# Attention and gated MLP on one core: the order of issue of all five engines is replaced

## The chip, the cores and the metric

The kernel runs on one core of one Trainium2 chip. The metric is the device time of one execution in microseconds (us), taken as the median of several executions. Five engines of the core matter: PE (TensorE: matmuls and transposes), DVE (VectorE), ACT (ScalarE), Pool (GpSimd, used here almost only to start transfers that add into what lies in SBUF), and SP (SyncE, which starts loads and stores). Each takes its instructions strictly in the order in which they were issued to it.

## What is computed

Attention over 8 batches of 8 heads, 576 tokens and 64 columns, then an MLP over the 4608 tokens of width 512. All inputs and outputs are fp32.

```python
def _attn_ref(q, k, v):
    q_d = q.reshape(B, H, Sd, factor, D).mean(axis=3)      # factor = 4, Sd = 144; k_d, v_d alike
    ...
    out_d = sm_attn(q_d, k_d, v_d)                         # full softmax attention of 144 x 144
    out_up = np.repeat(out_d, factor, axis=2)
    mask = np.abs(pos[:, None] - pos[None, :]) < factor    # a band of 7 keys for each token
    scores = np.where(mask, scale * np.matmul(q, k.transpose(0, 1, 3, 2)), -1000000.0)
    ...                                                    # softmax
    return out_up + np.matmul(attn, v)

def _moe_ref(x, w1, w2, w3, w_out):
    a = x @ w1
    b = x @ w2
    h = a * b @ w3
    return h @ w_out
```

## The kernel before

Every fp32 product of the MLP is made of three products of fp32r halves: a matrix is split into a rounded high half and the rest, its low half (`three()`, L310 to L312: high times high, high times low, low times high). w3 and w_out are first multiplied with each other (`fold`, products at L414, result split into `wphl`, L430), so that the MLP has three matrices left: two of gates and one down.

**Units and chunks.** Each batch is cut into 3 units of 192 tokens, 24 in all, and two units make a chunk of 384, 12 in all. `unit(n)` (batches 2 to 7) computes the band attention on DVE and ACT: seven products `pr` of q with shifted k (L860), their sums over 64 columns `s` (ACT L870, DVE L873), a softmax (L885 to L895), and seven products `pv` of weights and shifted v (ACT L918, DVE L926). The first of them is the accumulator `xl`. Three of the other six are added to it by DVE (L936) and three by a transfer that Pool starts and that adds in SBUF (L934), by turns, so each of Pool's additions stands between two of DVE's. There are 54 of them. Then `xl` is transposed (`xt`, L940), the pooled attention is added (L947) and x is split into `xh` and `xl` (L953, L954). The batches 0 and 1 take another way in groups (`pooled_sums`, `group_unit`, `group_scores` L745, `rest`, `group_values` L788), with PE making scores and values and DVE the sums of the softmax (`esm`, L770 to L772).

**Pooled attention.** `pooled(b)` needs sums of four neighbouring rows of q, k and v. SP loads the first quarter (`qks` L489, `vs` and `vl` L492 to L494) and Pool adds the three others by transfers (`qks` L507; v at L491 in three pieces, 72 and 56 rows into `vs` and 16 into `vl`). Each addition into a piece waits for the one before it into the same piece. `vl` is copied once by DVE for batches 0 and 1 (L511). `quad` then makes scores, exponentials and values on PE and ACT (L568, L583, L607, L529).

**Chunks of the MLP.** `moe(c)` runs over 8 slices of the hidden width. For each slice PE makes two gate products into `pab` (L310 to L312), ACT copies one (`a`, L1008), DVE multiplies the other in (L1010), ACT makes the high half `gh` (L1015) and DVE the low half `gl` (L1017). PE multiplies both down into `acc`, three banks at once; ACT copies them out (`o_sb`, L1029) and SP stores them (L1045, L1047).

**What sets the order.** All steps are first recorded in a `Plan` as tasks, each with its engine, its inputs and the buffers that it takes; `BUFS` says how many buffers each kind of tile has (3 `kv`, 3 `pv`, 2 `xl`, 1 `vs`, 1 `qks`). Then the table `ORDER` (L63 to L164) says for each engine in which order it takes its tasks. A number in it is the task's place in the order of recording on that engine:

```python
left[e] = [l[k] for w in ORDER[e].split() for a, _, b in [w.partition("-")] for k in range(int(a), int(b or a) + 1)][::-1]
```

The five orders are merged into one program order by a cost model in `Plan.order`; on each engine the order is the table's. The weights come as raw words through 4 buffers (`raw`, `words()`), which DVE and ACT convert (DVE L354, L357) and join, so SP's next weight load waits for a join.

Of the kernel before, what the change touches and what calls it, by code (L numbers as in the profile page):

```python
# [64 lines left out]
        "64 63 65-66 68 67 69 71 70 72-74 76 75 77-79 3 80 4 81-82 7 2 84 83 5 1 86 85 11 9 0 87 14 10 88-89 24 27 26 25 94 28 31 29 95 "  # L65
        "30 90 92 91 32 96 93 8 6 97-98 34 100 99 17 33 39 37 36 15 38 22 35 101 13 19 23 45 16 20 102 43 103 12 105 41-42 44 40 104 106 "
        "46 48 47 112 111 21 114-115 49 113 50 116 51 117 53-54 18 52 120 118-119 122 121 123 55 57-58 125 124 56 60 126 59 128 127 "
        "130-131 129 61 109 132-133 62 107 135 139 134 153 136 177 138 137 154 140 174 141 155 175 173 142 182 156 172 180 157 176 110 "
        "178 108 181 179 183 144 143 146 196-197 149 199 198 145 159 147-148 150 158 151 202 152 204-205 203 200 206 209 207-208 210-211 "
        "187 160 189 186 161 185 188 184 212 216 213-214 217 215 163 218 223 222 220-221 219 191 190 193 226 225 224 194 192 162 195 201 "  # L70
        "227-233 165 164 257 256 234 258 265 264 259-260 254 266 255 166 261 269 267 263 262 270 268 167 274 278 281 280 275 271 279 273 "
        "168 276 282 277 272 169 283-284 170 285 287 286 171 288-289 235 310 236 313 312 237 311 238-239 317 315 314 337 341 338 316 340 "
        "342 339 241 348 344-345 347 318 343 346 349 240 243 350-351 242 320-321 324 352 325 323 322 353-354 245 356 355 357-358 367 359 "
        "368 360 365 364 363 244 361 370 247 371 246 372 366 373 248 374 369 319 330 328 249 375 250 327 331 376-377 251 326 309 378 329 "
        "379-380 290 381 408 332 382-384 333 385 252 386 334 292 409 291 410 413 387 411 335 414 412 294 293 336 253 418 417 416 419 415 "
        "295 435 438 436 296 420 297 421-423 298 465 424-425 466 437 362 463 426 300 427-428 464 429 473 442 299 469 301 462 467 471 430 "
        "441 302 440 431-432 470 468 472 304 439 303 388 305 474-475 306 476 307 443 477-480 389 507 445 450 446 444 449 481 510 448 509 "
        "391 447 390 508 512 511 453 308 393 452 392 482 456 518 455 433 454 483-486 451 517 515 514 394 513 516 395 519 434 520-521 397 "
        "522 459 523-525 396 399 457 526-528 458 398 538 536 539 534 529 540 460-461 537 542 530 533 400 535 487 401-402 544 541 531 543 "
        "579 582 545 403 581 404 580 546-550 488 585 583 551 405 584 552 609 586 553 490 489 554 587 555 491 556-557 607 613 492 611 606 "  # L80
        "616 608 610 406-407 494 589 617 493 593 590 615 612 614 591-592 496 618 532 594 495 619-623 498 624 634 497 625-630 500 633 599 "
        "635 632 640 637 596 588 499 638 600 636 502 501 595 558 639 641 643 503 642 597-598 644 603 645 559 646-650 682 677 651 560-561 "
        "680 602 504 562 678 652 563 679 653 601 654-655 685 578 656 681 565 505-506 604-605 684 683 686 688 704-706 564 707 687 709 711 "
        "689-690 567 710 566 691-693 708 694-695 731 734 569 631 712 735 696-697 733 568 571 736 739 738 698 570 714 719 715 699-701 713 "
        "740 572 732 657 742 573-574 737 716 718 741 575-576 743 717 658-659 744-746 660 723 577 780 747 661 748-749 781 662 778 750-751 "
        "722 725 752-753 724 754-755 787 720 664 779 663 777 721 776 726 784 727 782 702 665-666 786 785 728 783 703 667 788 668 789-793 "
        "670 806-807 669 794-795 805 729-730 796-800 802 671-672 808 756 673 803 809 804 810 674 813 812 811 757 814-816 675 759 817 "
        "848-849 818 850 819 851 758 761 821 760 852 676 820 876 822-825 763 880 855 854 877 826 853 875 856 886 762 879 878 885 882 765 "
        "881 883-884 887 764 801 767 858 863 888-891 766 859 769 894-895 860 896-897 857 768 862 861 892-893 898 771 905 903 770 868 865 "
        "901-902 772 827 899 906 773-774 869 866 904 867 864 828 911 907-908 910 830 912 872 909 829 913 832 847 775 871 914-915 831 "  # L90
        "916-918 920 834 951 921 947 919 950 870 833 953 955 922-923 948 924-925 949 836 954 873 946 874 956 835 838 957 837 952 958 973 "
        "975-976 840 974 839 959-960 900 961 841 979 965-966 1001 977 967 842 968 978 926 843 1002 1004 980 962-963 1000 964 969 1003 "
        "981-982 1005 1009 927 1006-1007 844 970 1010 845 929 1008 846 1011 928 930-931 983 988 986 1012 984 1013-1015 985 987 1016 933 "
        "1050 932 993 934 1019 972 991 1046 1017 1048 1018 1020 1047 935 990 1052 1021-1022 936 1023 1049 1051 1024 971 992 937 989 1054 "
        "1056 1053 1045 1055 939 994 996 995 1057 938 940 997 941 998-999 1058-1060 942 1025 1061-1063 943-944 1064-1065 1076 1066-1067 "
        "1026 1075 1068 1080 1028 945 1073 1069 1027 1029 1081 1079 1030 1074 1078 1072 1071 1082 1031-1032 1077 1083-1085 1034 1033 "
        "1086-1088 1090 1089 1091 1036 1092-1095 1035 1037 1070 1038-1041 1096-1097 1099 1042-1043 1098 1101 1044 1100 1103 1102 1105 "
        "1104 1107 1106 1108-1109 1111 1110 1112-1114"
    ),
    DVE=(  # L100
        "71-75 1-2 5-7 77 76 78-79 3 0 4 80 22 8-10 81-83 12 11 13 15-16 23-25 29 14 30-32 36 17 85 84 86 19-20 37-39 21 87 18 43 88-89 "
        "52 90 26 51 53 91 54-55 44 56 96 92 94 97 93 58 57 59 98-99 45 33-34 46 100 27 60-62 35 101 28 102 50 103-106 40 111 113 95 112 "
        "41 115 114 116 42 47-49 117-118 180 63 119-120 64-65 122 181 123 121 184 66 124 185-186 125 67 127 126 68 165 69 129 128 70 166 "
        "130 179 107 182 167 172 183 173 136 131 174 168 175 149 132 134 201 133 150 195 135 137 202 151 190-192 138 109 194 196 198 197 "
        "108 153 169 110 187 208 170-171 199 176 139 177 209 178 188 193 141-142 152 200 140 189 215 144 143 220-222 146-147 145 154 148 "
        "223-225 216-217 155 203-204 156 226-228 157 205-207 229-230 210 231 211 219 212-213 159 214 158 218 232-234 252-255 160 259-262 "
        "161 266-269 256 273-274 257 235 258 275-276 263-265 162-163 270 164 271 280 272 281-282 277-279 283-287 304 236 305-306 237 "
        "307-308 238 316 318 320 239 319 317 321 323 322 309 240 324 326-327 325 328-330 242 331-332 311 241 333 310 312 336 243 345 347 "
        "349 244 313-315 334-335 348 338 246 346 350 352 245 337 339 248 351 247 353 355 354 341 356 249 357-358 250 359 340 251 360-362 "
        "389 391 364 393 390 363 366 288 392 342 394 396 289-290 367 365 395 397 399 291 369 400 292 398 401-403 418-420 368 293 430 294 "  # L110
        "431-432 404 295 405-406 433-436 343 437 296 344 370 421-422 409 407-408 371 423 298 297 411 299 438 440 412 300 410 414 439 "
        "441-444 301-302 372 303 445 413 446-447 450 448 475 477 479 424-426 476 449 373 480 478 482 481 427-428 374-375 415-416 377 429 "
        "483 485 452-453 376 451 486 484 455 378 487-488 379 454 489-491 494 503-505 492 380 507 381 506 493 508 510 417 456 383 382 "
        "496-497 509 548 457 549 384 511 385 513-514 550 512 495 386 515-517 499 387 458 388 518-521 498 523 551 560 552 562 564 561 553 "
        "459 565 500 522 461 566 563 462 567 525 460 526 555 554 463 524 556 568 528 570-571 501 569 465 527 572 464 573-577 589 466 578 "
        "557 467 591 590 593 558 580 579 468 592 469 594 596 502 582 595 529 471 581 470 530 597 599 472 583 585 473 598 474 559 600 531 "
# [1062 lines left out]
```

## Time and profile before

| | us |
|---|---|
| median of 3 runs | 765.7 (765.47 to 766.26) |
| the profiled execution, whole | 765.72 |
| span of its instructions | 763.9 |
| PE busy | 745.8 (98%) |
| DVE busy | 604.1 (79%) |
| ACT busy | 534.2 (70%) |
| Pool busy | 128.7 (17%) |
| granted TensorE clock, mean | 0.995 |

The times of the rows are of the profiled execution, in us from the start of its span. "Busy" counts instructions, not what they wait for. A row of a timeline says when an instruction starts, how long it takes and, in brackets, how long its engine had been idle before it and what released it. A chain of waits goes back from the last instruction, at each step to what released it; "issue" is time in which the engine waited for nothing that the profile shows. The granted clock is a share of full speed: 1.00 is 2.4 GHz, half of it 1.2 GHz.

### The profile page before, as it was taken

Reading aid. Unit: us, or ns where it says so; the run is one execution under the profiler, and the core shown is the slowest. Engines: PE = TensorE matmul, PEld = TensorE weight load, DVE = VectorE, ACT = ScalarE, POOL = GpSimd, SP = SyncE. Lnnn points to the kernel's source line nnn. Section 1 sums busy time; section 2 is a strip of 40 time slices with the busy share of each in tenths; the row PEclk is TensorE's granted clock in tenths of the full one; section 3 lists DMA queues with packets and bytes.
Section 4 is the critical chain, followed back from the end, with each engine's and each line's share of the span. In section 5 each row is a group of like instructions: output and inputs, shape, how many; then the busy total and the mean of one; then the engine's idle time right before and its main releaser. Section 6 shows DMA issues by size and latency. Waiting matters only on the chain.

```text
span 763.9 us, 14865 instructions
## 1 busy us (share of the span) xinstructions
PE 745.8 (98%) x5288; PEld 647.4 (85%) x5288; DVE 604.1 (79%) x1063; ACT 534.2 (70%) x2133; POOL 128.7 (17%) x163
## 2 busy tenths in 40 slices
PE   9999999999999998999999899999999999999995
PEld 5445788889999997899998799898999989999995
DVE  4856995649999997999999788999989989775121
ACT  5698778567887786878788677877885966852211
POOL 2030030300221222112122112102132211010000
PEclk9999999999999999999999999999999999999998
DMA  9988952653776577657585558755778365332101
GB/s 311 304 230 271 272 144 72 131 156 130 142 163 176 131 147 163 155 127 162 157 158 130 148 135 187 143 138 137 153 168 193 73 145 122 94 63 42 42 1 42
DMA packets 51462, 111.89 MB, mean 146 GB/s; under 512 B 5548, under 2 KB 19884, under 8 KB 51388
## 3 DMA queue, kind: packets, MB, share of 16 engines
q0 software_dynamic: 15360, 38.94, 30.2%
q1 hardware_dynamic: 35892, 71.75, 29.0%
q8 instruction: 41, 0.67, 0.4%
q14 instruction: 33, 0.27, 0.1%
q10 hardware_dynamic: 136, 0.26, 0.1%
HBM read 80.26 MB, written 9.44 MB: 117 GB/s over the span
## 4 chain that ended last, share of the span: by engine, by line
PE 68%; DMA 18%; DVE 5%; issue 5%; ACT 2%; POOL 1%; SPq 0%; POOLq 0%; DVEq 0%; ACTq 0%
PE pab L310 14%; PE pab L312 14%; PE pab L311 14%; PE acc L312 7%; PE acc L310 7%; PE acc L311 7%; DMA vs<-in_v_dram 4%; DMA raw<-in_w_dram 4%; DMA xl<-pv 3%; DMA vl<-in_v_dram 2%; DMA q<-in_qk_dram 2%; DMA qks<-in_qk_dram 2%; PE o_ps L529 2%; PE s_ps L568 1%; PE t_ps L607 1%
## 5 line engine op out<-in xcount | busy, mean ns | idle before, releaser
L918 ACT ACTIVATE pv<-kv,s 128x64 f32<-128x64 f32 x432 | 114.9, 338 | 19.5 <-DVE s L895 18.8
L870 ACT ACTIVATE junk<-pr 128x64 f32<-128x64 f32 x432 | 110.4, 255 | 17.5 <-DVE pr L860 8.1
L860 DVE TENSOR_TENSOR pr<-q_t,kv 128x768 f32<-128x768 f32 x126 | 116.5, 948 | 4.5 <-DMA kv<-in_kw_dram 4.0
L312 PE MATMUL acc<-wphl,gl 128*128 128x512 f32 x288 | 113.8, 395 | 3.2 <-DVE gl L1017 3.2
L310 PE MATMUL acc<-wphl,gh 128*128 128x512 f32 x288 | 114.5, 397 | 0.5 <-ACT gh L1015 0.5
L311 PE MATMUL acc<-wphl,gh 128*128 128x512 f32 x288 | 113.0, 392 | 0.0
L934 POOL DMA_DIRECT2D xl<-pv x54 | 48.8, 903 | 321.4 <-DVE xl L936 262.4
L1008 ACT COPY a<-pab 128x384 f32<-128x384 f32 x96 | 45.3, 472 | 68.4 <-PE pab L312 53.7
L873 DVE TENSOR_REDUCE s<-pr 128x12 f32<-128x768 f32 x90 | 84.1, 946 | 0.4
L1010 DVE TENSOR_TENSOR a<-pab,a 128x384 f32<-128x384 f32 x96 | 52.9, 551 | 39.4 <-PE pab L312 36.5
L870 ACT ACTIVATION_READ_ACCUMULATOR junk<-pr 128x1 f32 x432 | 81.1, 188 | 0.0
L1017 DVE TENSOR_TENSOR gl<-a,gh 128x384 fp32r<-128x384 f32 x96 | 52.7, 550 | 28.8 <-ACT gh L1015 28.7
L1015 ACT CAST gh<-a 128x384 fp32r<-128x384 f32 x96 | 48.7, 508 | 35.5 <-PE acc L311 23.2
L926 DVE TENSOR_TENSOR pv<-kv,s 128x768 f32<-128x768 f32 x72 | 67.7, 950 | 5.1 <-DMA xl<-pv 4.6
L312 PEld LDWEIGHTS acc<-wphl,gl 128*128 128x128 f32 x288 | 54.3, 188 | 16.1 <-DVE gl L1017 4.5
L310 PE MATMUL pab<-xh,wo 128*128 128x384 f32 x192 | 65.1, 339 | 1.5 <-ACT a L1008 1.5
L310 PE MATMUL pab<-xh,w1a 128*128 128x384 f32 x192 | 66.0, 344 | 0.0
L310 PE MATMUL pab<-xh,wb 128*128 128x384 f32 x192 | 65.9, 343 | 0.0
L491 POOL DMA_DIRECT2D vs<-in_v_dram x48 | 49.4, 1096 | 93.5 <-DMA vs<-in_v_dram 92.4
L310 PE MATMUL pab<-xh,w2a 128*128 128x384 f32 x192 | 65.2, 339 | 0.0
L312 PE MATMUL pab<-xh,wb 128*128 128x384 f32 x192 | 64.8, 337 | 0.0
L311 PE MATMUL pab<-xl,wb 128*128 128x384 f32 x192 | 64.7, 337 | 0.0
(120 smaller groups left out, 1754.5 us busy)
## 6 DMA issues: line engine op xcount, KB each, us to landing
xl<-pv POOLq DMA_DIRECT2D x54, 384.0 KB, 4.3
raw<-in_w_dram SPq DMA_DIRECT2D x32, 512.0 KB
qks<-in_qk_dram POOLq DMA_DIRECT2D x18, 576.0 KB, 7.4
kv<-in_kw_dram SPq DMA_DIRECT2D x18, 576.0 KB
kv<-in_vw_dram SPq DMA_DIRECT2D x18, 576.0 KB
out_dram<-o_sb SPq DMA_DIRECT2D x29, 256.0 KB
q_t<-in_q_dram SPq DMA_DIRECT2D x18, 384.0 KB
raw<-in_wout_dram SPq DMA_DIRECT2D x8, 512.0 KB
```

The source lines that it names most:

```text
L310: nc.tensor.matmul(out_ps, lhsT=lh, rhs=rh, start=first, stop=False)
L311: nc.tensor.matmul(out_ps, lhsT=lh, rhs=rl, start=False, stop=False)
L312: nc.tensor.matmul(out_ps, lhsT=ll, rhs=rh, start=False, stop=last)
L491: dma = (lambda **kw: nc.gpsimd.dma_start(accum_op=ALU.add, **kw)) if add else nc.sync.dma_start
L860: (nc.gpsimd if o in share["qk_pool"] else nc.vector).tensor_tensor(out=T[o], in0=T["q"], in1=T["k"][:, o * D:o * D + nq].rearrange("p (t ...
L870: nc.scalar.activation(out=junk, in_=T[o][:, t], func=AF.Copy, accum_out=T["s"][:, t, o:o + 1])
L873: reds.append(add("DVE", dve_us(nq), lambda o=o: nc.vector.tensor_reduce(out=T["s"][:, :, o], in_=T[o], op=ALU.add, axis=AX.X), [tp], uses ...
L918: nc.scalar.mul(out=T["pv", o][:, tt], in_=T["v"][:, (tt + o) * D:(tt + o + 1) * D], mul=T["s"][:, tt, o:o + 1])
L926: nc.vector.tensor_tensor(out=T["pv", o], in0=T["v"][:, o * D:o * D + nq].rearrange("p (t d) -> p t d", d=D), in1=T["s"][:, :, o].unsqueez ...
L934: t = add("Pool", 0.9, lambda o=o: nc.gpsimd.dma_start(out=T["x"], in_=T["pv", o], accum_op=ALU.add), [t, tm], uses=[hx, h], late=dma_us(1 ...
L1010: tg = add("DVE", dve_us(CT), lambda f=f: nc.vector.tensor_tensor(out=T["a", f], in0=T["p", 1, f], in1=T["a", f], op=ALU.mult), [ta, ends[ ...
L1017: tl = add("DVE", dve_us(CT), lambda f=f: nc.vector.tensor_tensor(out=T["gl", f], in0=T["a", f], in1=T["gh", f].bitcast(F32), op=ALU.subtr ...
```

## The change

Only the numbers in `ORDER` change, in all five lists. No task is added, removed or given to another engine. Moved are 594 of 807 tasks of PE, 913 of 1037 of DVE, 1028 of 1115 of ACT, 127 of 146 of Pool and 104 of 174 of SP, most of them by a few places. The first line of two lists:

```diff
     Pool=(
-        "0 2 5 3 1 4 6 9 7-8 13 12 16 10 15 18 11 19 14 17 23 20 27 21 31 24-25 28 41 29 32 45 33 22 26 34 30 35 49 36-37 42-43 38 44 48 "
+        "0 3 1-2 5-6 4 9 8 7 10 13 16 11 14 12 15 19 17-18 20-21 24 28 23 22 26 25 29 27 31 41 45 30 32 49 33-37 43-44 48 38 52 42 62 39 "
...
     SP=(
-        "13-16 0-1 17-20 2 21-22 3-5 23-26 12 27-38 6-7 39-40 8-9 41 59 42-43 60 10-11 44-46 56-57 47-48 61 64 58 62-63 68 49-52 81 65-67 "
+        "13-16 0 17-18 1 19-20 2 21-22 3-5 23-26 12 27-37 59 6-8 38-41 9-11 42-44 56 60 45-46 62 61 47-48 63 57-58 65 64 49-50 68 51-52 "
```

What the order looks like at four places follows. A row is one instruction, with its line, its kind, the tiles out<-in and the shape; the number behind a tile's name tells tiles apart within one kernel, and the two kernels number differently.

Pool at the start, the nine accumulations of batch 0's pooled v (`vs` in pieces of 72 and 56 rows, `vl` of 16 rows), before:

```order
L491 DMA vs_296<-in_v4_dram 56x512 x2
L491 DMA vl_297<-in_v4_dram 16x512
L491 DMA vs_296<-in_v4_dram 72x512 x2
L491 DMA vl_297<-in_v4_dram 16x512 x2
L491 DMA vs_296<-in_v4_dram 72x512
L491 DMA vs_296<-in_v4_dram 56x512
```

And after:

```order
L491 DMA vl_298<-in_v4_dram 16x512
L491 DMA vs_297<-in_v4_dram 72x512
L491 DMA vs_297<-in_v4_dram 56x512 x2
L491 DMA vl_298<-in_v4_dram 16x512
L491 DMA vs_297<-in_v4_dram 72x512
L491 DMA vl_298<-in_v4_dram 16x512
L491 DMA vs_297<-in_v4_dram 56x512
L491 DMA vs_297<-in_v4_dram 72x512
```

Of the three chains the short one on `vl` now starts first, and between two issues into the same piece stands an issue into another, except for one pair of 56 rows.

DVE at the start, around its copy of `vl` (L511); `raw`, `w3` and `wx` are weights being converted and joined, `esm` and `se` the softmax of a score group, `gsm` and `pexp` the pooled softmax. Before:

```order
L771 RECIPROCAL esm_271<-esm_271 128x6
L590 TENSOR_SCALAR gsm_497<-gsm_497 128x6
L591 RECIPROCAL gsm_497<-gsm_497 128x6
L598 TENSOR_TENSOR pexp_85<-pexp_85,gsm_497 128x3x16
L772 TENSOR_TENSOR se_322<-se_322,esm_324 128x432
L354 TENSOR_SCALAR raw_473<-raw_473 128x512
L772 TENSOR_TENSOR se_269<-se_269,esm_271 128x432
L357 SCALAR_TENSOR_TENSOR w3_562<-w3_562,raw_473 128x512
L511 COPY vl_297<-vl_297 16x512
L357 SCALAR_TENSOR_TENSOR w3_580<-w3_580,raw_535 128x512
L357 SCALAR_TENSOR_TENSOR w3_604<-w3_604,raw_541 128x512
L354 TENSOR_SCALAR raw_553<-raw_553 128x512
```

And after:

```order
L770 TENSOR_SCALAR esm_326<-esm_326 128x6
L771 RECIPROCAL esm_326<-esm_326 128x6
L511 COPY vl_298<-vl_298 16x512
L770 TENSOR_SCALAR esm_386<-esm_386 128x6
L771 RECIPROCAL esm_386<-esm_386 128x6
L772 TENSOR_TENSOR se_384<-se_384,esm_386 128x432
L770 TENSOR_SCALAR esm_269<-esm_269 128x6
L771 RECIPROCAL esm_269<-esm_269 128x6
L772 TENSOR_TENSOR se_267<-se_267,esm_269 128x432
L354 TENSOR_SCALAR raw_560<-raw_560 128x512
L357 SCALAR_TENSOR_TENSOR w3_621<-w3_621,raw_480 128x512
```

The copy stood among joins of weights; now the sums of two score groups stand directly behind it and the joins behind those.

DVE around the second of Pool's three additions into unit 9's `xl`. The first row is DVE's second addition into this unit's `xl`, which Pool's transfer follows, and the last row is DVE's third, which needs that transfer; `pr` and `s1` belong to unit 10, `gl` and `a` to the gates of a chunk. Before:

```order
L936 TENSOR_TENSOR xl_3393<-xl_3393,pv_3503 128x768
L873 TENSOR_REDUCE s1_80<-pr_3610 128x12
L873 TENSOR_REDUCE s1_80<-pr_3598 128x12
L926 TENSOR_TENSOR pv_3688<-kv_2991,s0_79 128x768
L1017 TENSOR_TENSOR gl_3683<-a_3580,gh_3682 128x384
L885 TENSOR_REDUCE mx_3705<-s1_80 128x12
L887 TENSOR_TENSOR s1_80<-s1_80,mx_3705 128x12x7
L1010 TENSOR_TENSOR a_3703<-pab_3601,a_3703 128x384
L936 TENSOR_TENSOR xl_3393<-xl_3393,pv_3635 128x768
```

And after, where DVE's second addition into this `xl` stands two rows above the first row shown:

```order
L926 TENSOR_TENSOR pv_3673<-kv_3016,s0_79 128x768
L926 TENSOR_TENSOR pv_3683<-kv_3016,s0_79 128x768
L954 TENSOR_TENSOR xl0_3644<-xt_3476,xh0_3643 128x4x192
L873 TENSOR_REDUCE s1_80<-pr_3613 128x12
L885 TENSOR_REDUCE mx_3717<-s1_80 128x12
L887 TENSOR_TENSOR s1_80<-s1_80,mx_3717 128x12x7
L1010 TENSOR_TENSOR a_3689<-pab_3663,a_3689 128x384
L892 TENSOR_REDUCE sm_3725<-s1_80 128x12
L894 RECIPROCAL sm_3725<-sm_3725 128x12
L895 TENSOR_TENSOR s1_80<-s1_80,sm_3725 128x12x7
L1017 TENSOR_TENSOR gl_3661<-a_3593,gh_3660 128x384
L936 TENSOR_TENSOR xl_3511<-xl_3511,pv_3673 128x768
```

Between the two additions there were seven rows, four of them long (two sums, one product, one `gl`); now there are twelve, among them two products, the `xl` of a finished unit, one sum and two `gl`.

Pool between 390 and 425 us of the trace; `xl_4786` before and `xl_4827` after are unit 13's accumulator, `xl_5084` and `xl_5203` unit 14's, and `vs_4993`, `vl_4994` before and `vs_4819`, `vl_4820` after are batch 5's pooled v. Before:

```order
L934 DMA xl_4786<-pv_4727 128x768
L507 DMA qks_4257<-in_qk4_dram 128x1152
L934 DMA xl_4786<-pv_4811 128x768
L934 DMA xl_4786<-pv_4956 128x768
L491 DMA vl_4994<-in_v4_dram 16x512
L491 DMA vs_4993<-in_v4_dram 72x512
L491 DMA vl_4994<-in_v4_dram 16x512 x2
L491 DMA vs_4993<-in_v4_dram 56x512 x2
L934 DMA xl_5084<-pv_5171 128x768
L934 DMA xl_5084<-pv_5265 128x768
```

And after:

```order
L934 DMA xl_4827<-pv_4751 128x768
L491 DMA vs_4819<-in_v4_dram 56x512
L491 DMA vs_4819<-in_v4_dram 72x512 x2
L934 DMA xl_4827<-pv_4922 128x768
L491 DMA vl_4820<-in_v4_dram 16x512 x2
L934 DMA xl_4827<-pv_5013 128x768
L934 DMA xl_5203<-pv_5115 128x768
L491 DMA vl_4820<-in_v4_dram 16x512
L507 DMA qks_5185<-in_qk4_dram 128x1152
L934 DMA xl_5203<-pv_5256 128x768
```

Unit 14's first addition stood behind six accumulations of v; now it stands directly behind unit 13's last one, and three accumulations into `vs` have moved ahead of unit 13's second addition.

## Rows read from the trace of the kernel before

**Rows 1.** The page's table of busy time, first line.
```profile
PE 745.8 (98%) x5288; PEld 647.4 (85%) x5288; DVE 604.1 (79%) x1063; ACT 534.2 (70%) x2133; POOL 128.7 (17%) x163
```
**Rows 2.** Stretches: length, busy PE, PEld, DVE, ACT, POOL, clock, DMA share, GB/s.
```profile
8.50:90.00 81.50, 78.48 (x632) 39.76 (x633) 60.06 (x151) 62.56 (x167) 7.65 (x9) 1.00 0.92 285
...
290.00:312.00 22.00, 19.97 (x157) 16.53 (x156) 17.59 (x27) 14.70 (x66) 4.37 (x5) 1.00 0.72 136
...
420.00:436.00 16.00, 13.33 (x88) 11.57 (x81) 11.07 (x17) 9.77 (x44) 2.54 (x3) 0.89 0.50 126
...
570.00:630.00 60.00, 59.34 (x404) 53.23 (x403) 52.99 (x87) 43.63 (x194) 11.90 (x14) 1.00 0.60 139
...
700.00:764.00 64.00, 56.20 (x293) 51.82 (x291) 13.61 (x23) 12.22 (x25) 0.00 (x0) 0.97 0.09 25
```
**Rows 3.** PE's waits: line, what it waited for, us in total, times, longest.
```profile
PE acc L312 <- DVE gl L1017: 3.2, 3, 2.7
...
PE se_ps L745 <- DMA k<-in_qk_dram: 0.8, 1, 0.8
PE oe_ps L788 <- DMA v_w<-in_v_dram: 0.8, 1, 0.8
PE se_ps L745 <- DVE se L756: 0.7, 2, 0.4
```
**Rows 4.** The chain of waits, 405 to 440 us: start, length, what.
```profile
414.89 1.12 POOL vs L491
416.01 3.87 issue
...
420.42 8.34 DMA xl<-pv
...
433.37 0.43 PE acc L311
...
436.08 0.23 PE acc L311
```
**Rows 5.** DVE's timeline, 414 to 434 us: start, length, instruction, wait ahead.
```profile
415.58 0.95 DVE L926 TENSOR_TENSOR pv<-kv,s 128x768 f32<-128x768 f32 x1
...
428.78 0.96 DVE L926 TENSOR_TENSOR pv<-kv,s 128x768 f32<-128x768 f32 x1 [4.04 <-DMA xl<-pv]
```
**Rows 6.** DVE's timeline, 286 to 306 us.
```profile
297.96 0.96 DVE L936 TENSOR_TENSOR xl<-xl,pv 128x768 f32<-128x768 f32 x1 [3.96 <-DMA xl<-pv]
```
**Rows 7.** The chain of waits of the whole span, two of its transfers.
```profile
263.20 4.27 DMA xl<-pv
...
290.01 7.93 DMA xl<-pv
```
**Rows 8.** DVE's timeline, 49 to 63 us.
```profile
59.13 0.42 DVE L511 COPY vl<-vl 16x512 f32<-16x512 f32 x1 [4.04 <-DMA vl<-in_v_dram]
```
**Rows 9.** Pool's timeline, 33 to 60 us.
```profile
37.45 0.84 POOL L491 DMA_DIRECT2D vs<-in_v_dram  x1 [2.90 <-DMA vs<-in_v_dram]
```
**Rows 10.** Stretches of the start, as in rows 2.
```profile
55.00:60.00 5.00, 5.00 (x20) 2.69 (x19) 0.93 (x3) 4.98 (x13) 2.25 (x3) 1.00 0.71 169
```
**Rows 11.** DVE's timeline, 654 to 657 us.
```profile
654.85 0.95 DVE L954 TENSOR_TENSOR xl<-xt,xh 128x768 fp32r<-128x768 f32 x1
```
**Rows 12.** PE's timeline, 655.8 to 656.6 us.
```profile
656.20 0.33 PE L310 MATMUL pab<-xh,w1a 128*128 128x384 f32 x1
```
**Rows 13.** Pool's timeline, 276 to 303 us.
```profile
288.03 0.87 POOL L507 DMA_DIRECT2D qks<-in_qk_dram  x1 [5.23 <-DMA qks<-in_qk_dram]
```
**Rows 14.** Pool's timeline, 396 to 412 us.
```profile
398.44 0.86 POOL L934 DMA_DIRECT2D xl<-pv  x1 [6.38 <-DVE xl L936]
...
409.12 0.78 POOL L491 DMA_DIRECT2D vl<-in_v_dram  x1 [3.17 <-DMA vl<-in_v_dram]
```
**Rows 15.** SP's timeline, 388 to 412 us.
```profile
390.80 0.61 SPq L1047 DMA_DIRECT2D out_dram<-o_sb  x1
...
402.00 0.37 SPq L492 DMA_DIRECT2D vs<-in_v_dram  x1
```

174 rows, old and new, of tables (ACT, DVE, PE, Pool) are left out of this document.

## The prediction

> **What bounds the kernel now.** I read the page's table of busy time first. TensorE (PE) is busy 745.8 of 763.9 us [rows 1], and no other engine comes near it, so the question is where the missing 18.1 us lie and whether an order can reach them. The stretches tell it [rows 2]: from 8.5 to 90 us PE is idle for 81.50 - 78.48 = 3.0 us, from 290 to 312 us for 2.0, from 420 to 436 us for 2.7, from 570 to 630 us for 0.7. From 700 us on it lacks 7.8, which is the output leaving after the last matmul; the 1.9 that are left stand mostly ahead of 8.5 us, where the first weights come in. So an order has 3.0 + 5.4 = 8.4 us of gaps to gain from, and the slow clock that one of them brings.
>
> Next come PE's waits [rows 3]. The largest is for the low half of the gate product (`gl`, on VectorE, DVE): 3.2 us in three waits, 2.7 of them in one. The chain of waits around 430 us shows its cause [rows 4]: Pool's queue stands for 3.87 us, then a transfer that adds a product into `xl` takes 8.34 us, then DVE can go on, and `gl` reaches PE only behind that. The matmuls behind the gap come 0.43 us apart, where the same kind comes 0.23 apart a little later [rows 4], and the granted clock of this stretch is 0.89 [rows 2]: PE ran at 1.2 GHz for a while and not at 2.4. A share of 0.11 of 16 us is 1.8 us, of which a little lies in the gap itself; I take 1.6. This one place costs 2.7 + 1.6 = 4.3 us.
>
> So PE sets the end, and it loses its time where an engine that takes its work in a fixed order stands behind a transfer.
>
> **The change, part by part.** No instruction is added or removed, and PE changes between fp32 and fp32r work as often as before (107 times, counted in both orders), so nothing is due for either. What changes is who stands behind whom.
>
> Around 416 us. Before, Pool issued v pieces of batch 5 ahead of unit 14's first `xl` addition, and the second of two 56-row pieces waited for the landing of the first; the addition stood behind it for 3.87 us. Now unit 14's first addition stands directly behind unit 13's last one. Its product was made at 415.58 + 0.95 = 416.5 us [rows 5], so it can go some 3.9 us earlier. Even if it takes 8.34 us again it lands 3.9 earlier, and of DVE's wait of 4.04 us [rows 5] 0.1 is left. The gap and its slow clock go: -4.3 us. What is late next is unit 13's transposed sum (`xt`), which DVE now has in that place; its transfer is issued one addition earlier, so it should be there.
>
> Around 298 us. DVE waits 3.96 us for unit 9's second addition [rows 6], which takes 7.93 us where another takes 4.27 [rows 7]. Between release and use the new DVE order has two long rows more (a `pv` product and the `xl` of a finished unit, 0.9 each from start to start), three rows of the softmax (0.25 each) and one `gl` (0.5), and one long row less: 1.8 + 0.75 + 0.5 - 0.9 = 2.1 us. Of 3.96 us 1.9 are left; PE's 2.0 us of idle time shrink in that proportion to 1.0: -1.0 us. The small waits between 570 and 630 us I leave as they are.
>
> The start. The steps of batch 0's attention move some three to five places forward on PE, and weight products whose inputs have long been there fill in behind. Two PE waits go: 0.8 for `v_w`, since SP now issues those loads ahead of three weight blocks, and 0.7 for `se` on DVE, since a weight product now stands between two score groups [rows 3]. One grows: the first score group comes one product (0.9) earlier, for a `k` that lands when it did, so 0.8 [rows 3] becomes 1.7. Denser transposes may cost 0.3. Sum: -0.8 - 0.7 + 0.9 + 0.3 = -0.3 us. One row of DVE goes both ways. Its copy of `vl` waited 4.04 us [rows 8] at the end of a chain of accumulations, in which the second issue stood 2.90 us for the first one's landing [rows 9] with two independent ones behind it; now the independent ones go first. That frees DVE some 4 us. But directly behind the copy now stands the sum of a score group (`esm`), whose exponentials ScalarE, busy 4.98 of 5 us there [rows 10], finishes near 59 us. So DVE stands as long as before, and the join of weight block 5 comes six rows or some 2 us later; with it a raw buffer and SP's next weight load. SP meanwhile issues four loads that came later before, some 2 us of traffic, so by count the first gates get their last weights when they did. The ends: -1.5 if DVE is simply freed, +2.5 if the join delays all gate weights. I take 0 between them.
>
> New waits. What cures two places can make others. By counting rows, the DVE work between release and use of the 54 additions is 8.4 us on average against 8.1, and five of those ahead of unit 23 had under 5 us before, three have now. Laying each of the 54 measured lengths against every spacing gives 10.5 us of waits for the old order and 9.4 for the new. Scaled so, 5.4 x 9.4 / 10.5 = 4.8 us would reach PE again; by the named places only 5.4 - 2.7 - 1.0 = 1.7 would be left. I take the middle, 3.3, which means 1.6 us of waits that the old trace does not show; the ends are 0 and 3.1.
>
> Does DVE keep up? Each chunk's x has to be ready when PE comes to its gates. The tightest is chunk 10: x is written at 654.85 + 0.95 = 655.80 and PE starts at 656.20 [rows 11, 12]. There the new order has 4.3 us less DVE work ahead (chunk 6: 8.9 less; chunk 3: 3.4 more, where 3.7 were to spare). So DVE can follow a PE that is 4 us ahead, and not one that is 10 ahead.
>
> Sum: -4.3 - 1.0 - 0.3 + 1.6 = -4.0 us. The profiled execution took 765.72 us (its span and 1.8 around it), as the median of 765.7 does, so the sum stands for both: 761.7. The 1.6 is the softest term, and I have seen the old order's bad places but not the new one's; I add 0.5 toward its upper end and forecast **762.2 us**.
>
> **What else could happen.** *The waits come back elsewhere.* The addition of 7.93 us ran beside an addition into `qks` issued at 288.03 [rows 13]; the one of 4.27 had none [rows 7]. The Trainium skill has this as a rule (DMA: Bandwidth & Descriptors, "Issuing engines are not separate DMA queues"): transfers that SP, ScalarE and GpSimd start run on the same 16 DMA engines and interleave. By that rule another place in Pool's queue moves a collision and does not remove it, and the two lengths agree. In that case 4.8 us reach PE again, one wait long enough to bring the slow clock (1.6): 4.8 + 1.6 against 5.4 + 1.6 is -0.6, and the start adds -0.3 to +0.5: **765.3 us**, no change.
>
> *Slower.* Pool now has two 72-row pieces of batch 5's v, the second waiting for the first, ahead of unit 13's second addition, which it issued at 398.44 before [rows 14]. They need SP's v load. That was issued at 402.00, and Pool went on with it at 409.12 [rows 14, 15], 7.1 us later. Now PE has batch 4's output 12.5 us earlier by its order, and SP has the store of 390.80 ahead [rows 15], so the load can start near 391 and land near 398. The first piece then lands near 403 (the one ahead of the 3.87 us took 5.0, from 414.89 to 419.88 [rows 4]), the addition near 407.5, and DVE, with 8.0 us of rows in between, wants it at 406.4: a wait of 1.1 that PE need not see, as 1.4 of the 4.04 were not seen. From there each us that the load lands later costs PE one. At 404 it costs 6 and the slow clock 1.6; with the -4.0 of the rest that is +3.6: about **769 us**. The weight joins at the start (+2.5) would push the same way.
>
> *Almost no new waits*, and a start that is freed: -4.3 - 1.0 - 1.5 = -6.8: **758.9 us**.
>
> **How the numbers follow.** Forecast 762.2, its own range 760.3 to 764.1: 0.50. No change near 765.3: 0.25. Slower, 767.2 to 771: 0.17. Near 758.9: 0.08. The range leaves out about half of the last case below and a half of the slow one above, some 0.12: 758.8 to 768.5. A measurement of this kernel tells about 0.2% (1.5 us) from no change, so the borders are 764.2 and 767.2: faster 0.50 + 0.08, same 0.25, slower 0.17.
>
> **What would show it.** Right: Pool's stand of 3.87 us ahead of unit 14's addition, PE's wait of 2.67 us for `gl` and the lower clock behind it are gone; PE idles some 1 us between 290 and 312 us; it comes to the first gates within 1.5 us of where it did before. Wrong: a new wait of PE of 2 us or more behind an `xl` addition, with the clock falling after it; unit 13's second addition issued after 404; the first gates more than 1.5 us later; or PE waiting for a chunk's x, which would mean that DVE and not PE is the bound.

## Result and profile after

The changed kernel took 756.81 us in the median (four executions, 755.33 to 759.28), beside 765.59 for the kernel before (four, 761.90 to 766.26): a ratio of 0.9898, with a 95% interval from 0.9855 to 0.9942. It is faster, as forecast, but 756.8 lies below the range of 758.8 to 768.5, and the 8.8 us are two and a half times the 3.5 of the forecast. Here and below, the ratios and intervals leave out the two slow executions (765.1 us of e6, 768.5 of the kernel before) and are not quotients of the medians, so the two can differ by some 1 us.

Later comparisons put this gap in another light. In all, 102 executions of the kernel before were timed beside the changed kernel and the experiments: they lie between 757.0 and 768.7 with a median of 762.3, and a fifth of them took 765.4 or more. All three that the forecast started from (765.47 to 766.26) belong to that fifth. Twelve more executions of the changed kernel (below) gave 756.72, with a ratio of 0.9939 (0.9912 to 0.9967). Put together, 762.3 against 756.7 is 5.6 us; in the one comparison that timed 29 executions of before beside those twelve it is 4.9.

The profiled execution of the changed kernel took 758.0 us, its span is 756.2, 7.7 less than before. The page's table of busy time and five stretches, which answer to [rows 1] and [rows 2] (length, busy PE, PEld, DVE, ACT, POOL, clock, DMA share, GB/s):

```profile
PE 741.5 (98%) x5288; PEld 646.5 (85%) x5288; DVE 608.0 (80%) x1063; ACT 534.8 (71%) x2133; POOL 128.4 (17%) x163
```

```profile
8.50:90.00 81.50, 78.85 (x639) 40.54 (x639) 63.27 (x154) 62.58 (x170) 7.64 (x9) 1.00 0.92 281
...
290.00:312.00 22.00, 22.00 (x182) 19.37 (x181) 20.95 (x33) 16.32 (x77) 4.67 (x7) 1.00 0.53 116
420.00:436.00 16.00, 16.00 (x86) 14.94 (x85) 14.91 (x26) 11.60 (x51) 4.36 (x5) 1.00 0.87 199
570.00:630.00 60.00, 60.00 (x351) 55.82 (x351) 52.60 (x85) 46.30 (x202) 11.16 (x14) 1.00 0.50 112
630.00:650.00 20.00, 18.27 (x138) 15.84 (x137) 15.83 (x24) 12.22 (x47) 2.50 (x3) 0.91 0.45 112
```

PE has no gap left from 290 to 312, from 420 to 436 and from 570 to 630 us, where it had 2.0, 2.7 and 0.7. A new one stands between 630 and 650 us, 1.7 us long and followed by the slow clock (a share of 0.09 of 20 us is 1.8 us). The chain of waits (start, length, what) shows a gap without a name, then the product of batch 7's probabilities and its pooled v, then gate matmuls 0.32 us apart, where 0.17 is the spacing at full clock:

```profile
635.39 1.73 issue
637.13 1.97 PE o_ps L529 x64
639.10 0.62 PE pab L310
639.72 0.32 PE pab L311
```

What PE waits for there is told by Pool's timeline, with the last accumulations of batch 7's v:

```profile
624.77 1.17 POOL L491 DMA_DIRECT2D vs<-in_v_dram  x1
629.93 1.69 POOL L491 DMA_DIRECT2D vs<-in_v_dram  x2 [3.99 <-DMA vs<-in_v_dram]
```

Three are left at 624 us, and the last two are issued after 629.93, behind a landing. In the kernel before the last was issued at 636.8 and PE came to the product at 648.0, 11 us later; now it is issued at 630.46 and PE stands ready at 635.4, 5 us later. The transfer took 6.6 us and so landed at 637.06, and PE started at 637.13. The order made PE ready 12.6 us earlier and the transfer only 6.3.

### The profile page after: what moved, and what is told of

It is laid out like the page before. It is cut to its first block, busy times and chain, and to the rows that moved or that the text cites. A ratio compares the mean times of both kernels' runs of the same rounds, so it can differ in the third digit from the quotient of the medians.

```text
span 756.2 us, 14865 instructions
## 1 busy us (share of the span) xinstructions
PE 741.5 (98%) x5288; PEld 646.5 (85%) x5288; DVE 608.0 (80%) x1063; ACT 534.8 (71%) x2133; POOL 128.4 (17%) x163
## 4 chain that ended last, share of the span: by engine, by line
PE 93%; DMA 4%; DVE 1%; ACT 1%; issue 0%; SPq 0%; DVEq 0%; ACTq 0%
PE pab L310 18%; PE pab L312 18%; PE pab L311 18%; PE acc L310 9%; PE acc L311 9%; PE acc L312 9%; PE accw L414 4%; DMA raw<-in_w_dram 4%; PE o_ps L529 2%; PE t_ps L607 2%; PE s_ps L568 2%; PE oe_ps L788 1%; PE se_ps L745 1%; PE te_ps L715 1%; DMA v_w<-in_v_dram 1%
## 5 line engine op out<-in xcount | busy, mean ns | idle before, releaser
L310 PE MATMUL pab<-xh,w1a 128*128 128x384 f32 x192 | 65.7, 342 | 0.0
L310 PE MATMUL pab<-xh,wo 128*128 128x384 f32 x192 | 65.3, 340 | 0.0
L312 PE MATMUL pab<-xh,wo 128*128 128x384 f32 x192 | 64.5, 336 | 0.0
L312 PE MATMUL pab<-xh,w1a 128*128 128x384 f32 x192 | 64.5, 336 | 0.0
L311 PE MATMUL pab<-xl,w1a 128*128 128x384 f32 x192 | 64.4, 336 | 0.0
```

What stands on the lines that cost most here:

```text
L310: nc.tensor.matmul(out_ps, lhsT=lh, rhs=rh, start=first, stop=False)
L311: nc.tensor.matmul(out_ps, lhsT=lh, rhs=rl, start=False, stop=False)
L312: nc.tensor.matmul(out_ps, lhsT=ll, rhs=rh, start=False, stop=last)
```

## Experiments

A PE step (a group of matmuls of one task) has a usual length for its kind, taken here as the tenth percentile of the spacing of its kind over all the profiles; what is longer is called lost time, and includes waits, the slow clock and the small costs of a change between kinds. The sum of a row accounts for its execution: the time of the execution less its lost time is 735.3 to 736.1 us in all fourteen. Summed over the stretches between points that both orders share, in us:

| profile | to first gates | chunk 0 | chunks 1-3 | 4-5 | 6-7 | 8-9 | 10-11 |
|---|---|---|---|---|---|---|---|
| before | 7.5 | 4.8 | 6.6 | 6.2 | 1.4 | 3.0 | 0.6 |
| before again (e1) | 8.4 | 4.9 | 6.2 | 2.7 | 1.4 | 2.6 | 0.6 |
| before a third time (e11) | 8.3 | 5.0 | 6.4 | 1.9 | 1.4 | 4.7 | 0.6 |
| before, unit 14's pair (e2) | 6.2 | 5.0 | 5.9 | 2.5 | 1.4 | 2.2 | 0.7 |
| before, unit 9's pair (e3) | 6.1 | 5.2 | 4.1 | 7.1 | 1.7 | 3.1 | 0.7 |
| before, both pairs (e6) | 4.2 | 4.6 | 4.0 | 2.1 | 1.4 | 2.3 | 0.6 |
| before, new start (e5) | 5.2 | 5.9 | 5.8 | 5.0 | 1.4 | 3.8 | 0.6 |
| after | 6.6 | 3.7 | 3.4 | 1.9 | 1.3 | 5.0 | 0.5 |
| after again (e7) | 6.9 | 3.8 | 3.1 | 2.7 | 1.3 | 7.2 | 0.5 |
| after, old start (e9) | 6.6 | 4.0 | 3.7 | 1.6 | 1.3 | 4.4 | 0.6 |
| after, v earlier (e4) | 7.4 | 3.8 | 2.9 | 1.9 | 1.3 | 3.1 | 0.6 |
| e4 and first 20 us old (e8) | 5.4 | 3.9 | 2.9 | 1.6 | 1.3 | 2.8 | 0.6 |
| the same again (e12) | 5.3 | 4.1 | 5.1 | 2.2 | 1.3 | 4.0 | 0.6 |
| e8 and `gl` earlier (e10) | 4.9 | 3.9 | 3.5 | 3.5 | 1.4 | 3.4 | 0.6 |

### Is it in each execution?

No edit: the kernel before again, twice.

> The kernel before, unchanged, for a second profile. If unit 9's transfer of 7.93 us and unit 14's blocked addition follow from the order of issue, both come again: VectorE waits 3 to 4 us for the addition into xl near 298 us and near 428 us, TensorE idles about 2.0 us in 290 to 312 and 2.7 us in 420 to 436, with a lower clock behind the second. Rival: the lengths of these transfers are chance; then at least one of the two waits is under 1 us in this profile and others stand elsewhere.

> The kernel before once more, unchanged, timed against itself and with a third profile. Theory (a profile is one draw): near 300 us TensorE loses 2 to 3 us again, since the addition into qks comes beside unit 9's second addition each time, while the 4.4 us near 430 us are there or not there, by whether the first 56-row piece takes over 4 us to land; the runs spread over 757 to 768. Rival (the waits are fixed by the order): both are there, and the runs lie within 2 us.

The two stretches of the second profile (one execution, 762.21 us), and of the third (761.88 in the median of twelve, 758.1 to 768.7, ratio 0.9988, 0.9960 to 1.0016):

```profile
290.00:312.00 22.00, 20.77 (x162) 17.54 (x161) 18.36 (x28) 15.32 (x69) 4.38 (x5) 1.00 0.74 153
420.00:436.00 16.00, 16.00 (x108) 14.03 (x107) 15.12 (x22) 12.27 (x58) 1.89 (x3) 1.00 0.67 161
```

```profile
290.00:312.00 22.00, 20.36 (x160) 17.13 (x159) 17.96 (x27) 14.93 (x68) 4.38 (x5) 1.00 0.73 144
420.00:436.00 16.00, 16.00 (x108) 13.92 (x107) 15.13 (x23) 12.21 (x58) 1.34 (x2) 1.00 0.70 176
```

The gap at 290 to 312 us comes each time (2.0, 1.2, 1.6 us, and 1.2 in each of e2 and e5, which keep this pair), the one at 420 to 436 us in neither. It hangs on one landing. Pool's wait for the first 56-row piece of batch 5's v was 2.53 us in the second profile and 2.40 in the third, where it had been 3.87:

```profile
419.22 0.83 POOL L491 DMA_DIRECT2D vs<-in_v_dram  x1 [2.53 <-DMA vs<-in_v_dram]
419.76 1.24 POOL L934 DMA_DIRECT2D xl<-pv  x1
```

Over the five profiles in which unit 14's addition stood behind that piece, it was issued 1.8 us (e1), 1.9 (e11), 3.6 (e5), 3.9 (before) and 4.2 us (e3) after its release, and chunks 4 and 5 lost 2.7, 1.9, 5.0, 6.2 and 7.1 us. Issued up to 1.9 us late the addition cost little, issued 3.6 to 4.2 us late it cost 3 to 5 us. So the mechanism of the forecast is right, and its price of 4.3 us is that of an unlucky execution; the mean of the five is 4.6 us, 2.4 above the 2.2 that the seven profiles of the new order lose there on average.

### One pair exchanged, unit 14

```diff
-86 84 90 94 85 89 80-82 95 88
+86 84 90 94 85 80 89 81-82 95 88
```

> The kernel before with one pair exchanged on GpSimd: unit 14's first addition stands ahead of the second 56-row piece of batch 5's v and not behind it. Theory (head of the queue): the addition is issued near 416.8 instead of 420.4 us, VectorE's wait of 4.04 us near 428 falls under 0.5, TensorE's 2.7 us of idle time and the half clock behind it go; 4.3 us less in a run that had the wait, 2 to 4.3 in the median. Rival (the transfer is long because of its neighbours on the DMA engines, not because it starts late): it takes even longer, now beside the v piece, VectorE still waits 2 us or more, and the time is unchanged.

The addition went at 415.67, as soon as its product was made, and the v piece behind it; chunks 4 and 5 lost 2.5 us and PE has no gap:

```profile
413.37 1.11 POOL L491 DMA_DIRECT2D vs<-in_v_dram  x1
415.67 0.92 POOL L934 DMA_DIRECT2D xl<-pv  x1 [1.19 <-DVE pv L926]
416.91 0.83 POOL L491 DMA_DIRECT2D vs<-in_v_dram  x1 [0.32 <-DMA vs<-in_v_dram]
```

The median is 760.87 against 763.03, ratio 0.9984 (0.9950 to 1.0017): too little to tell from none, as a gap that comes in some executions alone would give. By itself this run can't tell its theory from luck, since e1 and e11 lack the gap too; what the five above lost, by how late the addition went, speaks for the theory.

### One pair exchanged, unit 9

```diff
-40 53 62 66 54-55 51 70
+40 53 62 54 66 55 51 70
```

> The kernel before with one pair exchanged on GpSimd: the addition into qks that was issued at 288.0 us stands behind unit 9's second addition (290.0) and not ahead of it. Theory (collision): without the 576 KB beside it unit 9's addition takes 4 to 5 us and not 7.9, VectorE's wait of 3.96 us falls under 1, TensorE's 2.0 us of idle time between 290 and 312 us goes, and with it what follows at 303 to 313 (1.3 us); 2 to 3 us less in the median if the wait comes in each run. Rival (the length is chance, or the spacing of VectorE's rows alone decides): the addition takes 6 us or more, the wait stays over 2 us, and the time is unchanged.

Pool's timeline and VectorE's, with the addition into `qks` now behind:

```profile
289.58 0.86 POOL L934 DMA_DIRECT2D xl<-pv  x1 [9.08 <-DVE xl L936]
290.11 1.22 POOL L507 DMA_DIRECT2D qks<-in_qk_dram  x1
```

```profile
292.90 0.55 DVE L1010 TENSOR_TENSOR a<-pab,a 128x384 f32<-128x384 f32 x1
293.52 0.96 DVE L936 TENSOR_TENSOR xl<-xl,pv 128x768 f32<-128x768 f32 x1
```

DVE uses the sum 3.9 us after the issue and doesn't wait, where it waited 3.96 [rows 6], 3.30 and 3.69 us in the three profiles of before, 7.2 to 8.0 us after the issue. DVE's order is the same. PE is busy for all of the 22 us, while the other gap was there in this execution:

```profile
290.00:312.00 22.00, 22.00 (x186) 19.52 (x185) 21.60 (x34) 17.85 (x82) 5.66 (x7) 1.00 0.81 156
420.00:436.00 16.00, 13.09 (x57) 11.23 (x56) 11.49 (x17) 9.53 (x44) 0.89 (x1) 0.89 0.59 156
```

Median 760.95 against 763.03, ratio 0.9964 (0.9934 to 0.9994): the exchange of two numbers brings 2.1 us by the medians and 2.7 by the ratio, whose interval goes from 0.5 to 5. The neighbour made the transfer long, but not by running beside it: in e3 the addition into `qks` follows 0.5 us behind and does no harm; it harmed where it had been issued 2 to 3.5 us ahead. By the Trainium skill (DMA: Bandwidth & Descriptors, "Issuing engines are not separate DMA queues") transfers interleave on the same 16 DMA engines. That alone would leave the addition slow in either order, as the prediction's rival of returning waits had it; between these two, which Pool starts both, the traces show that the one issued first lands first. In the kernel before the addition into `qks`, issued at 288.03, landed after 8.0 us at 296.0 and unit 9's, issued at 290.01, at 297.9; in e3 unit 9's, issued at 289.58, landed at 293.5 and that into `qks`, issued at 290.11, at 297.8.

### Both pairs

The two diffs above together.

> The kernel before with both exchanges on GpSimd, of two neighbours each: unit 9's second addition ahead of the addition into qks, and unit 14's first addition ahead of the second 56-row piece. Theory (these two places cost 2 to 3 us in each run and 4.4 us in some): TensorE has no stall over 0.25 us near 300 and near 430 us, the median is 3.5 to 5 us under the kernel before's and the slowest runs, those over 765 us, are gone. Rival (the waits come back at other additions): 1 us or less, and runs over 765 stay.

Median 759.44 against 761.62, ratio 0.9959 (0.9927 to 0.9991), with executions from 753.6 to 765.1. The profiled one has a span of 753.1 and neither gap:

```profile
284.00:306.00 22.00, 22.00 (x173) 19.66 (x172) 21.59 (x32) 17.86 (x81) 5.23 (x6) 1.00 0.79 160
414.00:430.00 16.00, 16.00 (x106) 14.07 (x107) 15.01 (x24) 12.81 (x59) 0.91 (x1) 1.00 0.65 174
```

Four changed places in a table of thousands bring 2.2 us by the medians and 3.1 by the ratio (interval 0.7 to 5.6), about half of what the whole new table brings, but less than the 3.5 to 5 expected. The spread did not shrink as expected; one run over 765 stayed, and what such a run loses its time to is not shown.

### The start, alone and left out

e5: in each engine's list the tasks that start before the first gates take the order of the changed kernel, the others stay. e9: the reverse, on the changed kernel. PE's list:

```diff
 e5
-"15 17-19 16 20 22-23 21 25-27 24 0 30 29 28 31 35 34 1-2 32 3 33 ...
+"15 17 16 19 23 21 18 22 25 20 24 27 0 26 30 28 31 29 33 32 1 35 ...
```

> The kernel before, whose first 82 tasks of TensorE, 133 each of VectorE and ACT, 10 of GpSimd and 55 of SP (all that starts before the first gates, 86.7 us in its trace) stand in the order of the changed kernel, and all later ones as before. Four profiles with the old start lose 4.4 to 7.0 us of TensorE between 9 and 112 us in stalls over 0.25 us, the two with the new start 3.3 and 3.9. Theory (the start gains on its own, some 2 us): the first gates start 0.5 to 1.5 us earlier and the median is 1.5 to 2.5 us lower. Rival (the loads set the start, and my forecast of -0.3 stands): under 0.7 us.

> The changed kernel, whose first 82 tasks of TensorE, 133 each of VectorE and ACT, 10 of GpSimd and 55 of SP stand in the order of the kernel before; all later tasks stand as in the changed kernel. The counterpart of the run with the new start and the old rest, which had no gain. Theory (the start brings nothing, the rest brings all): the median stays at 756 to 757.5, TensorE has no stall over 0.5 us between 290 and 436 us, and the wait for o_ps at 635 us is there. Rival (the start brings the 1 to 2 us that its fewer stalls promise and the cut spoiled it in the other run): 758 to 759.

e5 has a median of 763.25 against 761.62, ratio 1.0021 (0.9995 to 1.0046); e9 758.84 against 762.53, ratio 0.9938 (0.9906 to 0.9969), the same as the changed kernel's own 0.9939, though its median lies in the range of its rival (758 to 759). The start brings nothing that can be measured. In lost time, the six profiles with the old start and old rest have 4.2 to 8.4 us to the first gates, 6.8 on average; the four with the whole new start 5.2 to 7.4, 6.5 on average: a gain of 0.3 in the stretch. The single stalls of before went and others came, as the first and third of these groups of PE's waits in the changed kernel show. The wait of 1.2 us for `wo` comes in every profile with the whole new start (0.7 to 1.3 us); the one of 1.8 for the first converted `w` is chance, since the old order has it too (1.8 us in e11):

```profile
PE accw L414 <- DVE w L357: 1.8, 1, 1.8
PE o_ps L529 <- issue: 1.7, 1, 1.7
PE accw L414 <- DVE wo L357: 1.2, 1, 1.2
```

### The new wait

e7 is the changed kernel again; e4 has three of batch 7's pieces earlier on Pool:

```diff
-127 124 126 130 136-138 131 135 134 139-145
+127 124 126 131 130 136-137 135 138 134 139-145
```

> The changed kernel, unchanged, for a second profile and a spread. If its wait of 1.73 us for o_ps near 635 us is a matter of the order, it comes again with the half clock behind it, and the median stays at 756 to 758. Rival (it is a matter of how long that chain's transfers take in a run): it is missing or under 0.5 us in this profile, and the times come in two heaps 2 to 3 us apart. The places that the old order lost time in (290 to 315, 420 to 436) should show no stall over 0.25 us in either case.

> The changed kernel with three accumulations of batch 7's pooled v issued earlier on GpSimd (each behind the landing that it needs, so that the last of them is issued near 625 and not at 630 us). Theory: TensorE's new wait of 1.73 us at 635 us, for o_ps of batch 7, and the half clock behind it are of that late chain; both go, and the time is 1.5 to 3.5 us under the changed kernel's, 753.5 to 755.5 in the median. Rival: the pieces then delay unit 21's additions into xl, VectorE waits there instead, and the time stays between 756 and 759.

The wait came again, longer, with a lower clock; PE's waits and the stretch in e7:

```profile
PE o_ps L529 <- issue: 2.4, 1, 2.4
```

```profile
630.00:650.00 20.00, 17.57 (x128) 14.62 (x128) 13.64 (x22) 10.62 (x42) 2.60 (x3) 0.83 0.45 112
```

In e4 the last piece goes at 625.18, and the stretch has its full clock; PE goes on from `acc` to `o_ps` without a gap:

```profile
630.00:650.00 20.00, 19.18 (x150) 16.08 (x149) 17.08 (x25) 13.20 (x52) 0.89 (x1) 1.00 0.35 99
```

What is left (0.8 us) is a wait for `gl`, which DVE makes behind a wait of 2.2 us for unit 21's last addition. e7 has a median of 756.72 (twelve, 754.7 to 761.0), e4 one of 755.61 (eight, 755.0 to 758.9), ratio 0.9897 (0.9861 to 0.9933) to the kernel before: the mechanism is shown, its worth about 1 us in the median, less than the 1.5 to 3.5 expected and not clear of noise (the changed kernel's ratios to before are 0.9898 and 0.9939). It cost 3.5 and 5.7 us of lost time in the two profiled executions of the changed kernel; that of e7 is the slowest of its twelve.

### A faster order?

e8 is e4 with the tasks of the first 20 us in the old order; e10 moves one more row of DVE, that `gl` ahead of the transpose that waits; e12 is e8 once more.

```diff
 e8
-"15 17 16 19 23 21 18 22 25 20 24 27 0 26 30 ...
+"15 17-19 16 20 22-23 21 25-27 0 24 30 ...
 e10
-982 905 944-945 874-875
+982 905 874 944-945 875
```

> The changed kernel with the three pieces of batch 7's v issued earlier, and with the tasks that start in the first 20 us in the order of the kernel before (13 of TensorE, 18 of VectorE, 14 of ACT, 16 of SP). Theory: the stalls of 2.1 to 2.3 us ahead of 17 us in the two profiles of the new start go to under 1, and the median falls to 753.5 to 755. Rival (the loads set when the gates come): the stalls move to between 40 and 90 us and the median stays at 755 to 756.

> The fastest order so far with one row of VectorE moved: the low half gl of chunk 9, slice 6, stands ahead of the transpose of unit 21's sum, which waits 2 us for an addition into xl, and not behind it. Theory: TensorE's stall of 0.87 us near 640 us goes (gh is ready at 636.1 us, gl is made by 637), nothing else moves, and the median is 0.5 to 0.9 us lower, 753.5 to 754. Rival: what stands behind (the x of chunk 10) is late instead and the median stays at 754.4.

> The fastest order so far (the changed kernel with the three pieces of batch 7's v earlier and the first 20 us in the old order) once more, since it had six runs only, 753.9 to 755.8. Theory (it lacks the wait at 635 us that the changed kernel has in each profile, and so the upper half of its spread): the median comes again at 754 to 755.5 and no run is over 758. Rival (the six were a lucky draw): the median is 756 to 757, as the changed kernel's own, with runs up to 760.

e8 came to 754.41 (six, ratio 0.9904, 0.9869 to 0.9938), e10 to 755.62 (six, 0.9889, 0.9863 to 0.9916), e12 to 756.94 (six, 0.9924, 0.9900 to 0.9947). So the 754.41 was a lucky draw, as e12's rival had it; over its twelve executions that order has 755.7, as e10 and e4 have. One stall that e8 was to remove, 1.2 to 1.3 us near 17 us in the two profiles of the changed kernel and in e4, is gone in e8, e12 and e10, but over e8 and e12 together the median is no lower than e4's. e10's `gl` did go earlier, at 638.35 and not behind the wait, but PE then waited 0.8 us for the next slice's `gh`, and the place lost 1.65 us in this profile where e4, e8 and e12 lost 0.87 to 1.09: no gain, as its rival had it, though by `gh` and not by the x of chunk 10. All 26 executions with the pieces of batch 7 earlier have a median of 755.7 (753.9 to 758.9), the 16 of the changed kernel 756.7 (754.7 to 761.0): about 1 us faster than it and 6.6 faster than before's 762.3, though these were not all timed in one comparison.

## Why the prediction was off

Two steps failed: the time that the sum started from, and the term around 298 us.

**The baseline.** The sum was made against one profiled execution of 765.72 us and a median of three that agreed with it within 0.8 us, and nothing in the range allowed for the kernel's own spread (a measurement was taken to tell 1.5 us). That spread is 11.7 us. The three were a high draw: 3.4 us above the later median, more than the whole distance from the range's lower end (758.8) to the result (756.8). From 762.3 the same sum gives 758.8 and the same range 755.4 to 765.1, which holds 756.8. By the later fifth three such draws in a row have a chance of about 1 in 125; whether something else made those three slow stays open.

**Around 416 us** (-4.3). Right in mechanism and, for this execution, in size: the 4.45 us of long stalls there are gone, and unit 14's addition went 0.3 us after its release (415.21 to 415.50). But as a difference of kernels the term is the mean of a chance, some 2.4 us.

**Around 298 us** (-1.0). The failed step of the mechanism: the transfer was taken to last 7.93 us again, so that more rows of DVE could cover only half of the wait. It lasted that long because Pool had started the addition into `qks` 2 us ahead of it [rows 7, 13], which the prediction had seen but kept for a rival. In the new order Pool issued that addition at 277.96, 9 us ahead of unit 9's. Unit 9's, issued at 286.86, took 4.2 us, and DVE used it at 292.71 without waiting. A second miss lies behind it: the stalls of 0.35, 0.70 and 0.28 us at 302 to 312 us were not booked to this place, though they came in all the profiles with the wait and in none without. In all 3.0 us went, and by the table 2.7 on average (6.2 in the five profiles of the old order without the exchange, 3.5 in the seven of the new order).

**The start** (-0.3). Right; a wash, as -0.8, -0.7, +0.9 and +0.3 had it. The 0.3 for denser transposes came from no row, and no run shows it; the whole stretch changed by -0.3 on average.

**Chunk 0**, 87 to 160 us, had no term, and loses 1.0 us less in the new order (3.7 to 4.1 in its seven profiles, 4.6 to 5.2 in the six of the old one). It is made of stalls of 0.3 to 0.6 us around the score groups of batch 1, each too small for the list of waits that was read. **570 to 630 us** was put at nothing without a reason, and its 1.4 us of stalls went. In the seven profiles with the old rest PE is idle there for 0.2 to 2.4 us, in the seven of the new order for nothing in six and 0.3 in one (e12). What cured it was not tested.

**New waits** (+1.6, and 0.5 more). They were sought by laying the lengths of 54 additions into `xl` against the rows between release and use. The one that came was of another kind, PE's own wait for `o_ps`: 3.5 and 5.7 us in the two profiles, and a gap of 1.6 without the slow clock in e9. The prediction knew that the pooled batches come earlier on PE, and priced Pool's v pieces against DVE for batch 5, but not against PE for batch 7.

**DVE keeps up.** Right: no wait of PE for a chunk's x is in the list of the changed kernel. **The slower rival** did not come: unit 13's second addition was issued at 393.79, well ahead of 404, since batch 5's v was loaded at 382.35 and not at 391. **The rival of waits that come back** was half right: a new wait came and brought the slow clock, but it was not behind an addition into `xl` and was smaller than what was gained.

So in the profiled pair the terms were -4.3 -1.0 -0.3 +2.1 = -3.5 and measured -4.4 -3.0 (290 to 315) -2.5 (long stalls to 90 us, a draw) -0.6 (chunk 0's long ones) -1.4 +3.5 and +0.7 of small ones: -7.7. As means over the profiles of the table, stretch by stretch, they are -0.3 -1.0 -2.7 -2.4 -0.1 +2.5 -0.1 = -4.1, beside 5.6 in the medians. The rest lies in which executions were profiled: the three of before average 763.9 us, 1.6 above their median, and the two of the changed kernel 759.5, 2.8 above theirs. These differ by 4.5 us, and so do their rows of the table.

## What to carry to other kernels

Take a second and a third profile of the kernel before when its time hangs on transfers: a gap that comes in each (a transfer that the order puts behind a larger one) is worth its length, a gap that comes in some (a queue that stands 2.4 to 4.6 us for a landing) only its share, and the spread of the runs belongs into the range. Look for what was issued ahead of a long transfer before you take its length along to a new order. When work is moved earlier on the busiest engine, go through every transfer that feeds it, not only the kind that hurt before.

## What the runs showed of the hardware

An addition in SBUF by a transfer of 384 KB took 7 to 8 us where Pool had started one of 576 KB 2 to 3.5 us ahead, and at most 3.9 where the same one came 0.5 us behind. At 632 us of the new order, where SP starts three loads within 1.3 us of it, it took 8.0 to 10.0 us in all seven profiles: 8.0 to 8.5 in the four with batch 7's pieces earlier, and 9.0 to 10.0 in the three in which Pool starts two v pieces within 2 us ahead of it. That these neighbours are the cause was not tested there.

A gap of PE of 1.63 us (e9, for `o_ps`) was followed by matmuls at the full clock, granted 1.00, and one of 1.73 us at the same place in the same order (after) by matmuls at 1.2 GHz, spaced 0.32 us and not 0.17, so that some 1.6 us more were lost. One gap can so cost double another that is 0.1 us shorter. The gap and the stretch in e9:

```profile
637.83 0.70 PE L531 MATMUL o_ps<-pt,vs 128*32 128x144 f32 x16 [1.63 <-issue]
```

```profile
630.00:650.00 20.00, 17.89 (x141) 14.75 (x141) 15.67 (x24) 12.59 (x49) 2.62 (x3) 1.00 0.45 112
```

The length of a gap does not decide it alone. A gap of 1.80 us at 9 us of the changed kernel's profile left the clock at 1.00 (the stretch from 8.5 to 90 us, above), and in e11 one of 1.60 us near 71 us was followed by the half clock (0.57 from 72 to 76 us):

```profile
9.07 6.65 PE L414 MATMUL accw<-wo,w 128*128 128x512 f32 x14 [1.80 <-DVE w L357]
```

```profile
71.03 1.32 PE L788 MATMUL oe_ps<-pte,v_w 72*32 72x64 f32 x80 [1.60 <-DMA v_w<-in_v_dram]
```

```profile
72.00:76.00 4.00, 4.00 (x33) 1.65 (x22) 2.38 (x6) 2.26 (x4) 0.00 (x0) 0.57 0.91 323
```
